# A turned table of weight scales, other transfer costs and a new table of key shifts in a planned attention-plus-FFN kernel

## The chip, the cores and the metric

The kernel runs on one core of a Trainium2 chip. Its metric is the time of one execution in microseconds (us) on that core, as the median of several runs. The engines are TensorE (PE in the profile; PEld is its loading of weights), VectorE (DVE), ScalarE (ACT), GpSimd (POOL) and SyncE (SP, which issues the transfers). Each engine takes its instructions in the order in which they were written into its queue and waits where an operand or a buffer isn't ready.

## The reference

Attention with a threshold (8 batches, 8 heads, 576 positions, head dimension 64), followed by a feed-forward network on 4608 tokens with 512 columns and 2048 hidden units:

```python
scores = scale * np.matmul(q, k.transpose(0, 1, 3, 2))
thresh = np.max(scores, axis=-1, keepdims=True) - tau
scores = np.where(scores >= thresh, scores, -1e9)
attn = np.exp(scores - np.max(scores, axis=-1, keepdims=True))
attn = attn / (np.sum(attn, axis=-1, keepdims=True) + 1e-09)
x = np.matmul(attn, v)              # then (tokens, 512)
h = x @ w_in                        # 512 -> 2048
g = np.where(h >= 1, h, np.where(h <= -1, 0, (h + 1) ** 2 / 4))
out = g @ w_out                     # 2048 -> 512
```

The weights arrive as 8-byte floats; the kernel first turns them into 4-byte floats and then splits them, like every other matmul operand, into a high and a low 2-byte float, so that two or three matmuls stand for one precise one.

## The kernel before

**Attention.** A tile is 128 rows of scores of one head (or 64 rows of each of two heads) against 576 keys; there are 288 tiles, 36 for each batch, and the tiles of a pair of heads form parts. For each tile PE computes the scores `s` (L836; two PSUM buffers, s_61 and s_62 in the order), DVE takes the maximum (L847 to L849), ACT the exponential (L852), DVE applies the threshold and sums (L856), DVE forms the factor (L860, L861), POOL multiplies by it (L864), ACT rounds to the high half (L869), POOL subtracts for the low half (L872), and a transposing transfer issued by SP (L875) writes `eT`. When all tiles of a part are there, PE multiplies by v (L942), and ACT and DVE write the result into the token buffer `x` (L950, L954).

**FFN.** It runs in steps. A step is one block of up to 256 tokens and some hidden units: PE's first matmuls (L1020), on ACT a relu and a square (L1026, L1029), on DVE the gate (L1033), ACT and DVE the halves of g (L1038, L1043), and PE's second matmuls (L1069), which add up in the one PSUM buffer `acc`. The first blocks hold 128 tokens, and a step of theirs has 48 first matmuls of 128 columns.

**Weights.** Each of the 32 blocks of weights (16 of w_in, in tile WI, and 16 of w_out, in WO) is loaded (L630), put together from two words on ACT (L642, L651) and DVE (L656, L660), measured by a small matmul (L667), scaled and split (POOL L721 or L713, PE L733 and L734, ACT L740 or DVE L738).

**Scales.** For w_in a small table `wsc_i` holds, for each of four groups of 512 hidden units, some powers of two; before, it is laid out with the kind of scale outside and the group inside. Once for each batch a block of DVE instructions (`f_scale`, L788 to L796) multiplies four-column rows of that table by the batch's own scale into `fcs`, which the FFN steps of that batch read as scale and bias. The relu of a batch's first step waits for it. Four of the nine instructions have four columns (L791, L793, L794, L795); the others have one. The four read a contiguous row of the table and write every fourth column of `fcs`.

**Order.** The program isn't written in the order in which it runs. Each piece of work becomes an operation with an engine, an estimated cost and a key; `Plan.order()` plays through them with those costs and, whenever an engine is free, takes the ready operation with the smallest key whose buffers are free. `Plan.key()` adds a shift from the table `SHIFT` to the key of single operations (of a kind and a number). Transfers carry a `work` cost in us, with which the planner keeps one clock for all transfers. What comes out is one fixed order for each engine.

Of the kernel before, what the change touches and what calls it, by code (L numbers as in the profile page):

```python
# [27 lines left out]
WL = 3.56  # L28
# [22 lines left out]
SHIFT = {  # L51
    "bits o": {7: -20, 8: -2, 12: -2},
    "den": {73: 5},
    "ffn": {8: 5, 12: -2, 19: 2, 21: -2, 22: -1.71, 23: -5},
    "ffn2": {1: 10, 9: -5, 10: 5, 16: 5, 18: -7.1, 19: -40, 23: -2, 24: 2, 25: -2, 26: -2},
    "load i": {0: -20, 1: -20, 11: -1.07},
    "load o": {8: 2},
    "load q k": {8: 4.48, 10: -4.1},
    "load v": {8: 19.78, 11: 5},
    "low o": {0: -19.88, 1: -18.87, 2: -16.6, 3: -10, 4: -10, 5: -5, 6: -5, 8: -2},  # L60
    "move": {8: -5, 9: -13.89},
    "norm": {39: -2, 58: -2, 69: -2},
    "parts o": {12: -2},
    "q k": {7: 20, 10: -5},
    "q k parts": {1: -8.79, 8: 5, 10: -5},
    "qk": {87: 25.43},
    "scale o": {0: -20},
    "send": {62: -5, 63: -10},
    "tile": {7: -2, 14: -2, 29: 5, 42: -2, 51: -2, 73: -10},
    "v": {1: 5, 2: 5},  # L70
    "v parts": {7: 17.66, 8: 35.35, 9: 33.43, 11: 11.83},
}
# [151 lines left out]
def attn_ffn_kernel(ctx: ExitStack, tc: tile.TileContext, qT, kT, vT, tau, w_in, w_out, out):  # L224
# [9 lines left out]
    NPAIR = H // 2  # L234
# [159 lines left out]
    def add_qk(b, p, need):  # L394
# [90 lines left out]
    def add_v(b, need):  # L485
# [3 lines left out]
        for p in range(NPAIR):  # L489
            rb = plan.buf("raw")  # L490
            bufs.append(rb)

            def load(rb=rb, p=p):
                Y.dma_start(ap(rb, raw), vT[b, 2 * p : 2 * p + 2].rearrange("h d s -> (h d) s"))

            def ssq(rb=rb, p=p):
                A.activation(junk, ap(rb, raw), AF.Square, accum_out=vssq[:, b, p : p + 1])

            l = plan.op("SP", 0.6, plan.key("load v", b * NPAIR + p, need - 8), load, take=[rb], work=1.1, behind=loads[-1] if loads else None)
            loads.append(l)  # L500
            squares.append(plan.op("ACT", 0.67, key - 5, ssq, [l], uses=[rb]))
# [75 lines left out]
    def w_scale(w, n, key, stats, gbuf):  # L577
        sb = plan.buf("ph")
        s = wsc[w][:, :, n]

# [23 lines left out]
    def add_w(w, keys):  # L604
        qn = NU // NQ[w]
        stats = []
        for u in range(NU):
# [82 lines left out]
        for u in range(NU):  # L690
# [5 lines left out]
            src, hi, lo = WT[w][:, u + WOFF, :], WTh[w][:, u, :512], WTh[w][:, u, 512:]  # L696
            s = wsc[w][:, 0, n : n + 1]
            how = CONV[w][u]
# [77 lines left out]
    def ends_():  # L776

        V.tensor_reduce(wsc["i"][:, 8, 0:1], wsc["i"][:, 0], AX.X, ALU.min)
        V.tensor_reduce(wsc["i"][:, 8, 1:2], wsc["i"][:, 1], AX.X, ALU.max)

    wends = plan.op("DVE", 0.13, KI[0] + KI[1] * (NU - 1), ends_, wscale["i"])
    fscale, oscale = {}, {}
    for b in range(B):
        s, f, wi, wo = scs[:, b, :], fcs[:, b], wsc["i"], wsc["o"]

        def f_scale(s=s, f=f, wi=wi):
            u, x, r, rx = (s[:, n : n + 1] for n in (4, 5, 6, 7))
            V.tensor_scalar(r.bitcast(U32), u.bitcast(U32), 1, None, ALU.logical_shift_right)  # L788
            V.tensor_scalar(rx.bitcast(U32), x.bitcast(U32), 1, None, ALU.logical_shift_right)
            V.tensor_scalar(s[:, 0:1], x, 2.0 ** -80, wi[:, 8, 0:1], ALU.mult, ALU.mult)  # L790
            V.tensor_scalar(f[:, :, 0], wi[:, 0], x, 2.0 ** -51, ALU.mult, ALU.mult)  # L791
            V.tensor_scalar(s[:, 0:1], s[:, 0:1], 1.0, 2.0 ** 66, ALU.min, ALU.mult)
            V.tensor_scalar(f[:, :, 1], wi[:, 3], r, 2.0 ** 88, ALU.mult, ALU.mult)  # L793
            V.tensor_scalar(f[:, :, 2], wi[:, 2], rx, 2.0 ** 37, ALU.mult, ALU.mult)  # L794
            V.tensor_scalar(f[:, :, 3], wi[:, 1], u, s[:, 0:1], ALU.mult, ALU.mult)  # L795
            V.tensor_scalar(s[:, 3:4], u, 2.0 ** 65, wi[:, 8, 1:2], ALU.mult, ALU.mult)  # L796

        def o_scale(s=s, wo=wo):
            V.tensor_scalar(s[:, 3:4], s[:, 3:4], 2.0 ** -15, wo[:, 1], ALU.max, ALU.mult)
# [333 lines left out]
```

## Time and profile before

| what | value |
|---|---|
| median of 3 runs | 1152.74 us (1152.41 to 1154.32) |
| the profiled execution | 1154.85 us, its span 1153.0 us |
| PE busy | 1104.0 us of the span (96%) |
| DVE, ACT, POOL busy | 950.2, 898.7, 799.8 us |
| mean granted TensorE clock | 0.986 of full speed |

Busy time of PE is modelled from pipelined matmuls, so it is no measure of how full PE is; the idle time beside it, and the chain of waits, tell where it had nothing to do. A tile's line numbers below are those of the kernel before. The change adds five lines above all the code in question, so that a line of the changed kernel has a number that is five higher (before L791, now L796).

### The profile page before, as it was taken

The numbers are of one execution on the slowest core, as the hardware profiler recorded it, in microseconds if no ns is written. First come the engines' busy times: TensorE is split into PE (matmuls) and PEld (weight loads), VectorE is DVE, ScalarE is ACT, GpSimd is POOL, SyncE is SP. The second block draws the span as 40 slices with busy tenths as digits, with TensorE's granted clock in tenths as the row PEclk, the third lists the DMA queues.
The fourth block names the chain that finished last, engine by engine and source line by source line (L and its number), as shares of the span: only waits on it lengthen the run. The fifth ranks groups of instructions, "written<-read, shape, count | busy, mean of one in ns | idle before, by whom it ended". The sixth has DMA issues, their size and how long they took to land.

```text
span 1153.0 us, 27218 instructions
## 1 busy us (share of the span) xinstructions
PE 1104.0 (96%) x9423; PEld 758.0 (66%) x9423; DVE 950.2 (82%) x2995; ACT 898.7 (78%) x1692; POOL 799.8 (69%) x957
## 2 busy tenths in 40 slices
PE   5789899999999999999999999999999999999998
PEld 3447556767677577676667667676678577676674
DVE  5899988988889989899789888888889889885241
ACT  6989777979788689787888879777888788785362
POOL 3678999588875788668966878758975898654000
PEclk8979999999999999999999999999999999999999
DMA  8798799879895899768995899668996798554000
GB/s 325 275 215 160 125 196 208 162 148 197 155 192 95 177 175 204 146 108 183 187 185 95 161 198 210 121 115 168 201 188 102 150 191 164 108 102 82 19 2 28
DMA packets 435929, 179.40 MB, mean 156 GB/s; under 512 B 400464, under 2 KB 407632, under 8 KB 435792
## 3 DMA queue, kind: packets, MB, share of 16 engines
q1 hardware_dynamic: 435792, 177.67, 76.0%
q8 instruction: 74, 1.21, 0.4%
q14 instruction: 63, 0.52, 0.2%
HBM read 45.09 MB, written 9.44 MB: 47 GB/s over the span
## 4 chain that ended last, share of the span: by engine, by line
PE 54%; DVE 16%; POOL 10%; ACT 8%; issue 6%; DMA 4%; SPq 1%; ACTq 0%; DVEq 0%; POOLq 0%
PE acc L1069 21%; PE ph L1020 20%; PE s L836 7%; PE ph L942 6%; POOL hl L872 3%; DVE e L856 3%; DVE sm L847 3%; POOL e L864 2%; POOL nat L457 2%; ACT e L852 2%; DVE ph L1033 1%; ACT junk L416 1%; DMA eT<-hl 1%; POOL raw L444 1%; DVE ga L1043 1%
## 5 line engine op out<-in xcount | busy, mean ns | idle before, releaser
L872 POOL TENSOR_TENSOR hl<-e,hl 128x576 f16<-128x576 f32 x286 | 366.6, 1286 | 98.7 <-ACT hl L869 95.2
L1020 PE MATMUL ph<-x,WI 128*128 128x256 f16 (+1 forms) x4032 | 401.6, 257 | 1.3 <-DVE gb L1043 0.6
L1020 PEld LDWEIGHTS <-WI 128*128 128x128 f16 x4032 | 346.4, 98 | 53.5 <-issue 5.7
L864 POOL TENSOR_SCALAR e<-e,sm 128x576 f32<-128x576 f32 x286 | 217.5, 765 | 113.0 <-DVE sm L861 76.7
L852 ACT ACTIVATE e<-s,sm,pc 128x576 f32<-128x576 f32 x288 | 237.7, 831 | 55.0 <-DVE sm L848 39.8
L856 DVE SCALAR_TENSOR_TENSOR e<-s,sm,e 128x576 f32<-128x576 f32 x288 | 231.4, 812 | 31.2 <-ACT e L852 24.8
L869 ACT ACTIVATE hl<-e 128x576 f16<-128x576 f32 x286 | 195.0, 684 | 61.0 <-POOL e L864 50.0
L847 DVE TENSOR_REDUCE sm<-s 128x1 f32<-128x576 f32 x288 | 215.6, 749 | 28.1 <-PE s L836 25.9
L836 PE MATMUL s<-kk,qq 128*128 128x288 f16 (+3 forms) x1360 | 193.2, 290 | 18.4 <-DVE e L856 12.5
L1069 PE MATMUL acc<-WO,ga 128*128 128x512 f16 x864 | 207.6, 381 | 0.8 <-ACT ob L1089 0.8
L836 PEld LDWEIGHTS <-qq 128*128 128x128 f16 (+3 forms) x1360 | 113.3, 100 | 94.1 <-issue 47.6
L1033 DVE SCALAR_TENSOR_TENSOR ph<-ph,fcs,asq 128x512 f32<-128x512 f32 (+1 forms) x160 | 112.0, 700 | 53.0 <-ACT asq L1029 52.1
L1026 ACT ACTIVATE asq<-ph,fcs 128x512 f32<-128x512 f32 (+1 forms) x160 | 116.2, 738 | 48.1 <-PE ph L1020 47.5
L1069 PEld LDWEIGHTS <-ga 128*128 128x128 f16 x864 | 81.7, 98 | 83.2 <-issue 4.8
L942 PE MATMUL ph<-eT,vst 128*64 128x320 f16 (+2 forms) x1928 | 124.6, 281 | 3.6 <-DVE WI L656 2.3
L942 PEld LDWEIGHTS <-vst 128*64 128x64 f16 x1928 | 99.3, 111 | 26.9 <-issue 17.4
L1029 ACT ACTIVATE asq<-asq 128x512 f32<-128x512 f32 x144 | 91.0, 632 | 2.1
L1038 ACT ACTIVATE ga<-ph,fcs 128x256 f16<-128x256 f32 (+1 forms) x160 | 70.3, 450 | 25.4 <-DVE ph L1033 23.2
L1043 DVE SCALAR_TENSOR_TENSOR ga<-ph,fcs,ga 128x256 f16<-128x256 f32 (+1 forms) x160 | 70.7, 450 | 21.0 <-ACT WO L1038 7.2
L1069 PE MATMUL acc<-WO,gb 128*128 128x512 f16 x300 | 73.3, 381 | 0.0
L457 POOL TENSOR_TENSOR nat<-raw,nat 128x576 f16<-128x576 f32 x56 | 71.6, 1289 | 1.8 <-ACT nat L450 1.7
L848 DVE TENSOR_SCALAR sm<-sm,pc 128x1 f32<-128x1 f32 x288 | 61.7, 214 | 10.4
(163 smaller groups left out, 1218.5 us busy)
## 6 DMA issues: line engine op xcount, KB each, us to landing
kk<-nat SPq DMA_DIRECT2D x112, 144.0 KB, 2.9
raw<-in_v_dram SPq DMA_DIRECT2D x32, 288.0 KB, 3.5
raw<-in_q_dram SPq DMA_DIRECT2D x32, 288.0 KB, 3.6
raw<-in_k_dram SPq DMA_DIRECT2D x32, 288.0 KB, 3.7
WO<-in_moe_w_in_dram SPq DMA_DIRECT2D x16, 512.0 KB, 8.2
out_dram<-ob SPq DMA_DIRECT2D x32, 256.0 KB, 2.6
qq<-nat SPq DMA_DIRECT2D x112, 72.0 KB, 2.3
x<-in_moe_w_out_dram SPq DMA_DIRECT2D x10, 512.0 KB, 6.0
```

What stands on the lines that cost most here:

```text
L836: T.matmul(ap(s, s_ps)[r, f, :SH], q, k, start=ql == kl == 0, stop=kl == 1)
L847: V.tensor_reduce(t[:, 0:1], sv(), AX.XY, ALU.max, negate=True)
L852: A.activation(halves(ap(e, es)[:, :S]), sv(), AF.Exp, bias=ap(m, sm)[:, 1:2], scale=ap(cb, pc)[:, 24 + v : 25 + v])
L856: V.scalar_tensor_tensor(halves(ap(e, es)[:, :S]), sv(), t[:, 2:3], halves(ap(e, es)[:, :S]), ALU.is_ge, ALU.mult, accum_out=t[:, 3:4])
L864: G.tensor_scalar(ap(e, es)[:, :S], ap(e, es)[:, :S], ap(m, sm)[:, 5:6], 1.0, ALU.mult, ALU.mult)
L869: A.activation(ap(x, hl)[:, :S], ap(e, es)[:, :S], AF.Copy)
L872: G.tensor_tensor(ap(x, hl)[:, w : w + S], ap(e, es)[:, :S], ap(x, hl)[:, :S], ALU.subtract)
L942: T.matmul(o[hd * D : (hd + 1) * D, :n], vt[:, k, hd * D : (hd + 1) * D], t[:, kb, hd * n : (hd + 1) * n], start=m == 0, stop=m == len(blo ...
L1020: T.matmul(h[:, i], WTh["i"][:, u, wl * 512 + c * P : wl * 512 + (c + 1) * P], x[:, cc, xl, c0 : c0 + n].rearrange("p (t n) -> p t n", n=P ...
L1026: A.activation(tv()[:, :, c], hv()[:, :, c], AF.Relu, bias=fcs[:, b, q, 2 : 3], scale=fcs[:, b, q, 1 : 2])
L1033: V.scalar_tensor_tensor(hv()[:, :, c], hv()[:, :, c], fcs[:, b, q, 0 : 1], tv()[:, :, c], ALU.max, ALU.min)
L1069: T.matmul(ap(ab, accs), gv(h, gl)[:, x], WTh["o"][:, fc + i, wl * 512 : (wl + 1) * 512], start=fc + i == 0 and m == 0, stop=fc + i == NFC ...
```

## The change

Three things change; the set of instructions on each engine stays the same in number and kind.

1. The table `wsc` has its two inner dimensions exchanged: the group is outside and the kind of scale inside. The four wide products of `f_scale` now read every ninth column of the table, where before they read four neighbours; they write every fourth column of `fcs`, as before. The two reductions over the groups read with a stride as well. The columns in which two extreme values are kept move along.
2. Costs that only the planner reads: the transfers of k and v 0.88 in place of 1.1, of a block of weights 1.55 in place of 1.75, and `f_scale` 1.2 in place of 1.4.
3. The table `SHIFT` is another one, with 111 entries for 24 kinds of work in place of 63 for 20.

```diff
 SHIFT = {
-    "load i": {0: -20, 1: -20, 11: -1.07},
...
+    "ffn": {3: -40, 4: -40, 5: -2, 7: 10, 11: 40, 17: 20, 19: -20, 20: -19.02},
...
-    wsc = {w: cp.tile([P, 9, NQ[w]], F32, name=f"wsc_{w}") for w in WT}
+    wsc = {w: cp.tile([P, NQ[w], 9], F32, name=f"wsc_{w}") for w in WT}
...
-        lk = plan.op("SP", 0.6, kl, load(kT, rk), take=[rk], work=1.1, behind=lq)
+        lk = plan.op("SP", 0.6, kl, load(kT, rk), take=[rk], work=0.88, behind=lq)
...
-            l = plan.op("SP", 0.6, plan.key("load " + w, u, key - WL), load, before, work=1.75)
+            l = plan.op("SP", 0.6, plan.key("load " + w, u, key - WL), load, before, work=1.55)
...
-        s = wsc[w][:, :, n]
+        s = wsc[w][:, n, :]
...
-        V.tensor_reduce(wsc["i"][:, 8, 0:1], wsc["i"][:, 0], AX.X, ALU.min)
-        V.tensor_reduce(wsc["i"][:, 8, 1:2], wsc["i"][:, 1], AX.X, ALU.max)
+        V.tensor_reduce(wsc["i"][:, 0, 8:9], wsc["i"][:, :, 0], AX.X, ALU.min)
+        V.tensor_reduce(wsc["i"][:, 1, 8:9], wsc["i"][:, :, 1], AX.X, ALU.max)
...
-            V.tensor_scalar(f[:, :, 0], wi[:, 0], x, 2.0 ** -51, ALU.mult, ALU.mult)
+            V.tensor_scalar(f[:, :, 0], wi[:, :, 0], x, 2.0 ** -51, ALU.mult, ALU.mult)
...
-            V.tensor_scalar(f[:, :, 1], wi[:, 3], r, 2.0 ** 88, ALU.mult, ALU.mult)
-            V.tensor_scalar(f[:, :, 2], wi[:, 2], rx, 2.0 ** 37, ALU.mult, ALU.mult)
-            V.tensor_scalar(f[:, :, 3], wi[:, 1], u, s[:, 0:1], ALU.mult, ALU.mult)
+            V.tensor_scalar(f[:, :, 1], wi[:, :, 3], r, 2.0 ** 88, ALU.mult, ALU.mult)
+            V.tensor_scalar(f[:, :, 2], wi[:, :, 2], rx, 2.0 ** 37, ALU.mult, ALU.mult)
+            V.tensor_scalar(f[:, :, 3], wi[:, :, 1], u, s[:, 0:1], ALU.mult, ALU.mult)
...
-        fscale[b] = plan.op("DVE", 1.4, k, f_scale, [VS[b], wends])
+        fscale[b] = plan.op("DVE", 1.2, k, f_scale, [VS[b], wends])
```

Three places of the orders follow; a line of three dots stands for rows left out.

First, DVE at the `f_scale` of the first batch. sm_124 and its like are the small results of one tile, e_94 its exponentials; WO<-x_105 joins two words of a weight. Before:

```order
L656 SCALAR_TENSOR_TENSOR WO<-x_106,ph_65 128x512
...
L856 SCALAR_TENSOR_TENSOR e_94,sm_125<-s_62,sm_125,e_94 128x576
...
L791 TENSOR_SCALAR fcs<-wsc_i,scs 128x4
L792 TENSOR_SCALAR scs<-scs 128x1
L793 TENSOR_SCALAR fcs<-wsc_i,scs 128x4
L794 TENSOR_SCALAR fcs<-wsc_i,scs 128x4
L795 TENSOR_SCALAR fcs<-wsc_i,scs 128x4
...
L847 TENSOR_REDUCE sm_126<-s_61 128x1
```

Now:

```order
L784 TENSOR_REDUCE wsc_i<-wsc_i 128x1
L661 SCALAR_TENSOR_TENSOR WO<-x_105,ph_63 128x512
...
L796 TENSOR_SCALAR fcs<-wsc_i,scs 128x4
L797 TENSOR_SCALAR scs<-scs 128x1
L798 TENSOR_SCALAR fcs<-wsc_i,scs 128x4
L799 TENSOR_SCALAR fcs<-wsc_i,scs 128x4
L800 TENSOR_SCALAR fcs<-wsc_i,scs 128x4
...
L852 TENSOR_REDUCE sm_124<-s_61 128x1
```

The block stood between the fourth tile's threshold and the fifth tile's maximum; it stands ahead of the third tile's maximum now.

Second, PE at the ninth and tenth tile (tile 8 in s_61, tile 9 in s_62; both from kk_78 and qq_82). Before:

```order
L836 MATMUL s_61<-kk_78,qq_82 128x288
...
L667 MATMUL acc<-WO 128x128
L733 MATMUL ph_65<-WI,dgw_132 128x512
L734 LDWEIGHTS minus
L734 MATMUL ph_65<-WI,minus 128x512
...
L836 MATMUL s_62<-kk_78,qq_82 128x288
...
L942 MATMUL ph_63<-eT_99,vst_88 64x128
```

Now:

```order
L672 MATMUL acc<-WO 128x128
L738 MATMUL ph_64<-WI,dgw_132 128x512
L739 LDWEIGHTS minus
L739 MATMUL ph_64<-WI,minus 128x512
...
L841 MATMUL s_61<-kk_78,qq_82 128x288
...
L841 MATMUL s_62<-kk_78,qq_82 128x288
...
L947 MATMUL ph_64<-eT_99,vst_88 64x128
```

The weights' matmuls stood between the scores of the two tiles; they stand ahead of both now.

Third, PE from the third FFN step on (L1020, now L1025; 48 matmuls each). Before:

```order
L1020 MATMUL ph_65<-x_103,WI 128x128
...
L836 MATMUL s_61<-kk_78,qq_82 64x288
...
L1020 MATMUL ph_63<-x_103,WI 128x128
L733 MATMUL ph_64<-WO,dgw_134 128x512
...
L836 MATMUL s_62<-kk_80,qq_84 128x288
```

Now:

```order
L1025 MATMUL ph_63<-x_103,WI 128x128
...
L841 MATMUL s_62<-kk_80,qq_84 128x288
...
L738 MATMUL ph_65<-WI,dgw_133 128x512
...
L1074 MATMUL acc<-WO,ga_110 128x512
...
L841 MATMUL s_61<-kk_79,qq_83 128x288
...
L947 MATMUL ph_63<-eT_99,vst_88 64x320
...
L1025 MATMUL ph_65<-x_103,WI 128x128
```

The fourth step followed the third after the scores of two tiles; now the scores of twelve tiles, the matmuls of the weights and the second matmuls of the first three steps lie between them.

More of the change, by code (lines that the diff above doesn't have):

```diff
@@ L51 @@
 SHIFT = {
[L52 to L55, printed above, removed]
-    "load i": {0: -20, 1: -20, 11: -1.07},
[L57 to L71, printed above, removed]
+    "av": {3: -80, 6: -20, 9: -67.64, 14: 20, 18: 40},
+    "bits o": {15: -20},
+    "den": {33: -80, 35: -40, 38: -10, 41: -2},
+    "ffn": {3: -40, 4: -40, 5: -2, 7: 10, 11: 40, 17: 20, 19: -20, 20: -19.02},
[9 rows of a table added]
+    "move": {5: 17.57, 6: 20},
+    "norm": {7: -2, 12: -10, 13: -20, 14: -20, 16: -40, 20: -20, 31: -80, 38: -2, 43: 5, 59: 5},
[6 rows of a table added]
+    "tile": {13: -2, 14: -5, 36: 10, 42: -2},
+    "v": {1: -1.03, 2: 20},
+    "v parts": {4: -2, 9: 16.66},
+    "x": {10: -5},
 }
@@ L497, in ssq @@
                 A.activation(junk, ap(rb, raw), AF.Square, accum_out=vssq[:, b, p : p + 1])
-            l = plan.op("SP", 0.6, plan.key("load v", b * NPAIR + p, need - 8), load, take=[rb], work=1.1, behind=loads[-1] if loads else None)
+            l = plan.op("SP", 0.6, plan.key("load v", b * NPAIR + p, need - 8), load, take=[rb], work=0.88, behind=loads[-1] if loads else None)
             loads.append(l)
@@ L696, in add_w @@
             src, hi, lo = WT[w][:, u + WOFF, :], WTh[w][:, u, :512], WTh[w][:, u, 512:]
-            s = wsc[w][:, 0, n : n + 1]
+            s = wsc[w][:, n, 0:1]
             how = CONV[w][u]
@@ L789, in f_scale @@
             V.tensor_scalar(rx.bitcast(U32), x.bitcast(U32), 1, None, ALU.logical_shift_right)
-            V.tensor_scalar(s[:, 0:1], x, 2.0 ** -80, wi[:, 8, 0:1], ALU.mult, ALU.mult)
-            V.tensor_scalar(f[:, :, 0], wi[:, 0], x, 2.0 ** -51, ALU.mult, ALU.mult)
+            V.tensor_scalar(s[:, 0:1], x, 2.0 ** -80, wi[:, 0, 8:9], ALU.mult, ALU.mult)
+            V.tensor_scalar(f[:, :, 0], wi[:, :, 0], x, 2.0 ** -51, ALU.mult, ALU.mult)
             V.tensor_scalar(s[:, 0:1], s[:, 0:1], 1.0, 2.0 ** 66, ALU.min, ALU.mult)
[L793 to L796, printed above, removed]
+            V.tensor_scalar(f[:, :, 1], wi[:, :, 3], r, 2.0 ** 88, ALU.mult, ALU.mult)
+            V.tensor_scalar(f[:, :, 2], wi[:, :, 2], rx, 2.0 ** 37, ALU.mult, ALU.mult)
+            V.tensor_scalar(f[:, :, 3], wi[:, :, 1], u, s[:, 0:1], ALU.mult, ALU.mult)
+            V.tensor_scalar(s[:, 3:4], u, 2.0 ** 65, wi[:, 1, 8:9], ALU.mult, ALU.mult)
         def o_scale(s=s, wo=wo):
-            V.tensor_scalar(s[:, 3:4], s[:, 3:4], 2.0 ** -15, wo[:, 1], ALU.max, ALU.mult)
+            V.tensor_scalar(s[:, 3:4], s[:, 3:4], 2.0 ** -15, wo[:, 0, 1:2], ALU.max, ALU.mult)
         k = start[b, 0] + 6
-        fscale[b] = plan.op("DVE", 1.4, k, f_scale, [VS[b], wends])
+        fscale[b] = plan.op("DVE", 1.2, k, f_scale, [VS[b], wends])
         oscale[b] = plan.op("DVE", 0.13, k, o_scale, [fscale[b]] + wscale["o"])
```

15 rows, old and new, of the table SHIFT are left out of this document.

## The prediction

> **What bounds the kernel now.** I read the page first, then busy times by stage, then the chain of waits, then single engines at the places where the chain leaves PE.
>
> The page's row for the engines, and a table of stages (start and end, length, then busy us and instructions of PE, PEld, DVE, ACT and POOL, the granted clock, the transfers' share and GB/s):
>
> ```profile
> PE 1104.0 (96%) x9423; PEld 758.0 (66%) x9423; DVE 950.2 (82%) x2995; ACT 898.7 (78%) x1692; POOL 799.8 (69%) x957
> ```
>
> ```profile
> 0.00:24.00 24.00, 10.43 (x65) 7.91 (x66) 11.68 (x39) 16.91 (x36) 9.11 (x43) 0.96 0.91 339
> 24.00:92.00 68.00, 53.51 (x390) 29.62 (x389) 60.81 (x190) 61.01 (x118) 44.20 (x64) 0.81 0.86 250
> 92.00:216.00 124.00, 115.88 (x1182) 79.87 (x1182) 111.48 (x360) 100.74 (x190) 113.33 (x134) 1.00 0.93 172
> 216.00:384.00 168.00, 167.88 (x1485) 118.27 (x1483) 151.32 (x490) 142.19 (x271) 128.12 (x148) 1.00 0.81 152
> 384.00:408.00 24.00, 21.80 (x150) 12.90 (x149) 20.02 (x62) 14.37 (x27) 14.73 (x14) 0.93 0.89 197
> 408.00:600.00 192.00, 187.85 (x1529) 129.52 (x1527) 167.88 (x528) 157.45 (x294) 151.74 (x178) 1.00 0.87 170
> 600.00:1130.00 530.00, 529.21 (x4553) 372.26 (x4552) 425.93 (x1327) 404.09 (x760) 338.56 (x381) 1.00 0.68 131
> 1130.00:1153.00 23.00, 17.48 (x81) 7.63 (x78) 1.13 (x4) 1.92 (x5) 0.00 (x0) 0.97 0.08 24
> ```
>
> PE is idle for 1153.0 - 1104.0 = 49.0 us. The change moves no work on or off PE, so the time changes by what this idle time changes. It lies in 0 to 24 (13.6 us), 24 to 92 (14.5), 92 to 216 (8.1), 384 to 408 (2.2), 408 to 600 (4.2) and at the very end (5.5, the last eviction and store, which no order helps). From 216 to 384 and from 600 to 1130 PE misses 0.9 us in all: what an order does there is worth nothing.
>
> Up to 24 us everything waits for v and the first weights, and both orders begin alike. From 24 to 92 us DVE (60.8 of 68) and ACT (61.0) set the pace, since PE has no FFN work before the weights are ready. From 92 to 216 us POOL does (113.3 of 124).
>
> The chain of waits (start, length, what), at the pieces that the change touches:
>
> ```profile
> 58.75 0.57 DVE fcs L791
> 59.36 0.62 DVE fcs L793
> 59.98 1.24 DVE fcs L794
> 61.22 0.19 DVE fcs L795
> ...
> 73.33 0.97 PE acc L667 x8
> 74.30 1.81 PE ph L733 x2
> 76.12 0.43 PE ph L734
> 76.54 0.92 PE s L836 x6
> ...
> 124.02 1.21 DVE fcs L794
> 125.23 1.11 DVE fcs L795
> ```
>
> ```profile
> 385.84 1.75 DVE fcs L791
> ...
> 390.04 0.65 PE s L836 x4
> ```
>
> The four-column products of `f_scale` are on the chain three times. They shouldn't be: they handle four numbers for each partition. The instructions in order of time show why they are long:
>
> ```profile
> 58.60 1.36 POOL L721 TENSOR_SCALAR WI<-WI,wsc_i 128x512 f16<-128x512 f32 x2
> 58.66 0.65 DVE L791 TENSOR_SCALAR fcs<-wsc_i,scs 128x4 f32<-128x4 f32 x1
> 59.22 0.14 DVE L792 TENSOR_SCALAR scs<-scs 128x1 f32<-128x1 f32 x1
> ...
> 59.88 1.34 DVE L794 TENSOR_SCALAR fcs<-wsc_i,scs 128x4 f32<-128x4 f32 x1
> 59.92 1.27 POOL L872 TENSOR_TENSOR hl<-e,hl 128x576 f16<-128x576 f32 x1
> ```
>
> L794 ends at 61.22, POOL's L872 at 61.19; L791 ends at 59.31, and POOL's two L721 together at 59.96, so the first of them at about 59.3. A four-column product lasts until POOL's instruction of that moment is over; the one-column L792 between them is not held (0.14). Where POOL doesn't interfere, the same products take this:
>
> ```profile
> 894.34 0.21 DVE L793 TENSOR_SCALAR fcs<-wsc_i,scs 128x4 f32<-128x4 f32 x1
> 894.47 0.22 DVE L794 TENSOR_SCALAR fcs<-wsc_i,scs 128x4 f32<-128x4 f32 x1
> 894.60 0.28 DVE L795 TENSOR_SCALAR fcs<-wsc_i,scs 128x4 f32<-128x4 f32 x1
> ```
>
> One starts 0.13 us after the other.
>
> **The change part by part.** The turned table. It takes away nothing by itself; what it can do is end the holding. Its two ends: if a product with a stride on both sides isn't held, it costs its 0.13 us (L795 0.19, as on the chain at 61.22). First batch: 0.57 + 0.62 + 1.24 - 3 x 0.13 = 2.0 us. Second batch: 1.21 + 1.11 - 0.13 - 0.19 = 2.0 us. Batch at 385.84: 1.75 - 0.13 = 1.6 us, and there PE itself stood still behind it:
>
> ```profile
> 390.04 0.65 PE L836 MATMUL s<-kk,qq 128*128 128x288 f16 x4 [2.20 <-DVE e L856]
> ```
>
> Together 5.6 us; the five other batches' blocks lie in stretches in which PE doesn't wait. The other end is 0: the products are held as before. For the upper end speaks that a one-column product beside them is free, so that holding hangs on the shape of the operands, and the operand that was contiguous is the one that changes; against it, that the output had a stride already. No row shows a product with two strides. I take the 5.6, as only slightly likelier than 0, since it decides more of the result than any other term.
>
> Planner's costs and keys. They do nothing on the chip but set the order. I counted, for fixed points of the program, the instructions ahead of them on an engine in both orders. Four things follow.
>
> (a) Two waits of DVE between 24 and 92 us:
>
> ```profile
> 44.55 0.69 DVE L656 SCALAR_TENSOR_TENSOR WI<-WO,ph 128x512 uint32<-128x512 uint32 x1 [1.79 <-ACT ph L651]
> ...
> 77.49 0.76 DVE L847 TENSOR_REDUCE sm<-s 128x1 f32<-128x576 f32 x1 [1.13 <-PE s L836]
> ```
>
> The second is the second place of the order: between the scores of tiles 8 and 9 PE did 0.97 + 1.81 + 0.43 = 3.2 us of weights' matmuls, and DVE waited for tile 9. With both tiles' scores side by side that work is behind DVE's work on tile 8, so 1.13 us go. The first: ACT came late with a word of one of the last blocks of w_in. In the new order ACT's L651 of these blocks stand further ahead (the fifteenth is ACT's instruction 50, before 59), so I take its 1.79 us as gone too. Together 2.9 us, between 0 and 2.9 us if something else is late there.
>
> (b) What DVE has to do before the first FFN step. It can begin when `x` has been written by the fourth L954. Ahead of that now stand one L528 (the low half of a later batch's v), one L656, one L660 and five operations of one column more, and the maximum, mask and four small operations of one tile less; the small ones cancel to within 0.1 us:
>
> ```profile
> L528 DVE SCALAR_TENSOR_TENSOR vb<-raw,scs,vb 128x576 f16<-128x576 f32 x28 | 35.6, 1272 | 0.3 <-POOL vb L523 0.2
> L656 DVE SCALAR_TENSOR_TENSOR WI<-WO,ph 128x512 uint32<-128x512 uint32 x11 | 7.4, 681 | 3.3 <-ACT ph L651 3.3
> L847 DVE TENSOR_REDUCE sm<-s 128x1 f32<-128x576 f32 x288 | 215.6, 749 | 28.1 <-PE s L836 25.9
> L856 DVE SCALAR_TENSOR_TENSOR e<-s,sm,e 128x576 f32<-128x576 f32 x288 | 231.4, 812 | 31.2 <-ACT e L852 24.8
> ```
>
> 1.27 + 2 x 0.68 - 0.75 - 0.81 = 1.1 us later (L660 does the same columns as L656 and is taken as equal). Behind L954 PE waits with the first L1020.
>
> (c) The first `f_scale` moves ahead of the third tile. All of its nine instructions come before tiles 2 and 3 and not after; DVE does the same sum, and the first relu that needs it is far behind in both orders. Its cover is that DVE never idles there, so I count 0.
>
> (d) The FFN steps behind the third. This is the third place of the order. Ahead of the first scores of the second batch (tile 36) stood seven steps' first matmuls (336), and now stand five (240), with as many second matmuls (36); one pair of L733 and L734 less as well. What moves behind, by the same work where it stood before:
>
> ```profile
> 104.43 2.84 PE L1020 MATMUL ph<-x,WI 128*128 128x128 f16 x48
> ...
> 110.04 2.85 PE L1020 MATMUL ph<-x,WI 128*128 128x128 f16 x48
> 112.73 1.08 PE L733 MATMUL ph<-WO,dgw 128*128 128x512 f32 x2
> ...
> 118.87 1.12 PE L733 MATMUL ph<-WO,dgw 128*128 128x512 f32 x2 [1.82 <-DVE x L954]
> ```
>
> 2.84 + 2.85 + 1.1 = 6.8 us of PE's work. If tile 36 comes when it came before, PE has idled that much longer, and from 216 us on it has no slack to make it good: 6.8 us is the upper end. The lower end is 0, if the attention comes that much sooner. For POOL, which paces 92 to 216, exactly the same instructions stand ahead of the low half of tile 36 in both orders, and POOL idles only 124.0 - 113.3 = 10.7 us there. But what stands ahead of the earlier tiles on POOL is more now (at the seventeenth low half one L457, one L523 and two L864), so that some of POOL's later work is done in its idle time before 92 us (24.0 - 9.1 and 68.0 - 44.2, together 38.7 us). That leaves room to come sooner by most of 6.8 us. I take 1.8 us, a wait as the longest of PE's in that stretch.
>
> Sum: -5.6 - 2.9 + 1.1 + 1.8 = -5.6 us. The profiled execution, 1154.85 us (its span and 1.85 us around it), would become 1149.2; it was 2.1 us above the median of the runs, so for the median 1152.74 - 5.6 = 1147.1 us.
>
> [...]
>
> **The rivals.** The products are held as before. Mechanism: a stride on one operand didn't free them, so neither does a stride on the other, and each of the four still lasts until POOL's current instruction ends. For it speaks L794's 1.34 us with its strided output; against it only that a second stride is new. Time: -2.9 + 1.1 + 1.8 = 0.0, so 1152.7 us, no change; it can go either way by a us or two, since the blocks meet POOL at other moments.
>
> PE runs short between 92 and 216 us (slower). Place: behind the third FFN step. The price is the full 6.8 us in place of 1.8. It decides from the point at which tile 36 comes no sooner than before. For it speaks that POOL has the same work ahead of that tile, and that DVE and ACT have little slack before 92 us (7.2 and 7.0 of 68 us); against it POOL's idle 38.7 us. With the products held: -2.9 + 1.1 + 6.8 = +5.0, 1157.7 us. With the products free it would be -0.6, no change.
>
> The order's gain isn't there. The waits of (a) go but others come, and the products are free: -5.6 + 1.1 + 1.8 = -2.7, 1150.0 us. It is the upper part of the forecast's own range.
>
> **How the numbers follow.** Of a single measurement, 0.2% (2.3 us) is about what can be told from no change. Forecast (products free, a modest price in (d)): 0.44, nearly all of it faster by more than 2.3 us (0.41), the rest within; its own range is 1143 to 1151. Products held: 0.28, within 2.3 us mostly (0.15), faster 0.07, slower 0.06. PE short: 0.28, slower 0.25, within 0.03. Sums: faster 0.48, same 0.21, slower 0.31. The range must reach to the last case: 1142 to 1158 us; about 0.1 is left out on either side.
>
> **What would show it.** The products: their groups' means near 0.2 us and none of them on the chain, or means of 0.4 to 0.7 as now. (a): no wait of DVE for L651's or PE's scores above 1 us between 24 and 92 us. (d): PE's busy time from 92 to 216 us, 115.9 now; below 112 would show the second rival, and 216 to 384 us would again have no idle time. PE's idle time over the span, 49.0 us now, must fall to about 43. The forecast is wrong if this idle time grows, or if it falls while the groups' means of the products stay.

## The result and the profile after

The change makes the kernel slower. Beside each other on the chip the changed kernel took 1159.9 us (median of 4 runs, 1155.65 to 1161.56) and the kernel before 1152.6 us (4 runs, 1151.54 to 1154.32); the ratio is 1.0053, with a 95% interval of 1.0032 to 1.0074. The prediction had said 1147.1 us, and 1159.9 lies above its whole range.

The profiled execution of the changed kernel is the shortest of its four (1155.65 us, span 1153.9 us). It is used for where waits lie and how long they are; times are compared by the ratios. The page's row of engines, after:

```profile
PE 1098.7 (95%) x9423; PEld 758.2 (66%) x9423; DVE 957.1 (83%) x2995; ACT 901.5 (78%) x1692; POOL 797.7 (69%) x957
```

PE's idle time, which the prediction wanted to see fall from 49.0 to about 43 us, has grown to 1153.9 - 1098.7 = 55.2 us. The span of these two profiles grew by 0.9 us only, since PE's busy time, which is modelled, is 5.3 us less here for the same 9423 matmuls. So the idle time shows where PE waits, and isn't by itself the size of the loss. Where PE is idle, the table of stages after says (the columns as in the prediction's table):

```profile
24.00:92.00 68.00, 47.26 (x384) 26.36 (x385) 63.19 (x195) 61.23 (x119) 45.61 (x65) 0.77 0.85 253
92.00:216.00 124.00, 113.37 (x1138) 77.08 (x1137) 113.19 (x354) 99.59 (x184) 115.06 (x145) 0.97 0.86 170
384.00:408.00 24.00, 22.58 (x159) 14.16 (x158) 22.92 (x76) 16.90 (x33) 17.84 (x23) 1.00 0.85 164
408.00:600.00 192.00, 190.31 (x1562) 132.93 (x1560) 165.54 (x522) 159.15 (x297) 150.38 (x177) 1.00 0.86 176
600.00:1130.00 530.00, 527.88 (x4549) 371.80 (x4548) 428.08 (x1334) 405.11 (x758) 338.89 (x382) 1.00 0.67 131
```

From 24 to 92 us PE idles 20.7 us where it idled 14.5, although DVE does more there (63.19 us for 60.81). From 92 to 216 us it idles 10.6 for 8.1 us, and from 600 to 1130 us 2.1 for 0.8. It is better from 384 to 408 us, 1.4 for 2.2 us, and from 408 to 600 us, 1.7 for 4.2 us.

Of the long waits of PE from 24 us on that the kernel before hasn't got, these four are followed below, in order of time; two more (2.30 us at 30.31 us and 2.42 us at 171.67 us) are not. A second profile of the same program, taken later, has neither the wait at 171.67 us nor the one at 151.26 us:

```profile
58.12 0.61 PE L672 MATMUL acc<-WO 128*128 128x128 bf16 x4 [6.05 <-DVE WO L661]
99.34 1.81 PE L947 MATMUL ph<-eT,vst 128*64 128x128 f16 x30 [2.58 <-DVE wsc_o L327]
151.26 1.63 PE L841 MATMUL s<-kk,qq 64*128 64x288 f16 x12 [2.84 <-DVE e L861]
915.24 0.65 PE L841 MATMUL s<-kk,qq 128*128 128x288 f16 x4 [1.84 <-DVE e L861]
```

All four end with DVE. What DVE does ahead of the first of them, with POOL's instructions of the same moment between (instructions of both engines in order of time, changed kernel):

```profile
52.77 1.22 DVE L799 TENSOR_SCALAR fcs<-wsc_i,scs 128x4 f32<-128x4 f32 x1
52.80 1.16 POOL L718 TENSOR_TENSOR WI<-WI 128x512 f16<-128x512 f32 x1
53.90 1.32 DVE L800 TENSOR_SCALAR fcs<-wsc_i,scs 128x4 f32<-128x4 f32 x1
53.91 1.28 POOL L462 TENSOR_TENSOR qq<-raw,qq 128x576 f16<-128x576 f32 x1
...
55.25 0.74 DVE L852 TENSOR_REDUCE sm<-s 128x1 f32<-128x576 f32 x1
...
56.35 0.75 DVE L852 TENSOR_REDUCE sm<-s 128x1 f32<-128x576 f32 x1
...
57.39 0.68 DVE L661 SCALAR_TENSOR_TENSOR WO<-x,ph 128x512 uint32<-128x512 uint32 x1
```

Two things are to be seen. The products are held as before: L799 ends 0.03 us after POOL's L718, L800 0.03 us after L462, with a stride on both operands. And the first `f_scale`, which now stands ahead of the third tile's maximum, takes from 51.33 to 55.33 us, 4.0 us; the word of w_out (L661) that PE's small matmul L672 wants comes behind it and two tiles' maxima, and PE, which takes its instructions in order, stands for 6.05 us.

### The profile page after: what moved, and what is told of

Same layout as the page of the kernel before. It is cut to its first block, busy times and chain, and to the rows that moved or that the text cites. A ratio compares the mean times of both kernels' runs of the same rounds, so it can differ in the third digit from the quotient of the medians.

```text
span 1153.9 us, 27249 instructions
## 1 busy us (share of the span) xinstructions
PE 1098.7 (95%) x9423; PEld 758.2 (66%) x9423; DVE 957.1 (83%) x2995; ACT 901.5 (78%) x1692; POOL 797.7 (69%) x957
## 4 chain that ended last, share of the span: by engine, by line
PE 62%; DVE 14%; POOL 6%; issue 4%; ACT 4%; DMA 2%; SPq 1%; ACTq 0%; POOLq 0%; DVEq 0%
PE acc L1074 24%; PE ph L1025 22%; PE s L841 8%; PE ph L947 7%; DVE e L861 3%; DVE sm L852 3%; POOL hl L877 2%; POOL e L869 2%; DVE ph L1038 1%; POOL nat L462 1%; DVE ga L1048 1%; ACT e L857 1%; DVE sm L853 1%; ACT hl L874 1%; DMA eT<-hl 1%
## 5 line engine op out<-in xcount | busy, mean ns | idle before, releaser
L877 POOL TENSOR_TENSOR hl<-e,hl 128x576 f16<-128x576 f32 x286 | 367.1, 1290 | 107.8 <-ACT hl L874 105.6
L1025 PE MATMUL ph<-x,WI 128*128 128x256 f16 (+1 forms) x4032 | 402.7, 258 | 0.7 <-DVE x L959 0.7
L1025 PEld LDWEIGHTS <-WI 128*128 128x128 f16 x4032 | 348.1, 98 | 52.9 <-issue 5.2
L869 POOL TENSOR_SCALAR e<-e,sm 128x576 f32<-128x576 f32 x286 | 216.5, 762 | 109.0 <-DVE sm L866 81.9
L861 DVE SCALAR_TENSOR_TENSOR e<-s,sm,e 128x576 f32<-128x576 f32 x288 | 230.7, 812 | 24.7 <-ACT e L857 17.9
L841 PE MATMUL s<-kk,qq 128*128 128x288 f16 (+3 forms) x1360 | 188.1, 291 | 11.1 <-DVE e L861 8.5
L462 POOL TENSOR_TENSOR nat<-raw,nat 128x576 f16<-128x576 f32 x56 | 71.1, 1282 | 2.4 <-ACT nat L455 2.3
```

Source lines behind the costliest of these rows:

```text
L841: T.matmul(ap(s, s_ps)[r, f, :SH], q, k, start=ql == kl == 0, stop=kl == 1)
L861: V.scalar_tensor_tensor(halves(ap(e, es)[:, :S]), sv(), t[:, 2:3], halves(ap(e, es)[:, :S]), ALU.is_ge, ALU.mult, accum_out=t[:, 3:4])
L869: G.tensor_scalar(ap(e, es)[:, :S], ap(e, es)[:, :S], ap(m, sm)[:, 5:6], 1.0, ALU.mult, ALU.mult)
L877: G.tensor_tensor(ap(x, hl)[:, w : w + S], ap(e, es)[:, :S], ap(x, hl)[:, :S], ALU.subtract)
L1025: T.matmul(h[:, i], WTh["i"][:, u, wl * 512 + c * P : wl * 512 + (c + 1) * P], x[:, cc, xl, c0 : c0 + n].rearrange("p (t n) -> p t n", n=P ...
```

## The experiments

The first theory, formed from these rows: the turned table does nothing, and the order loses, because the `f_scale` blocks now stand ahead of work for which PE waits and are lengthened by POOL. The rival: the table itself costs. In all the runs below a kernel is timed in five rounds beside the kernel before.

### The two halves of the change

Table alone: the kernel before with the new layout of `wsc`, the old keys and costs. Order alone: the new keys and costs with the old layout.

```diff
-    wsc = {w: cp.tile([P, 9, NQ[w]], F32, name=f"wsc_{w}") for w in WT}
+    wsc = {w: cp.tile([P, NQ[w], 9], F32, name=f"wsc_{w}") for w in WT}
```

> The kernel before with the turned table alone; order and costs are the old ones. Theory (the loss lies in the order): no change, 1152.6 us within 2 us, and the four-column products still last until POOL's instruction ends, with group means of 0.4 to 0.7 us as before. Rival (the table itself costs, because a strided source makes the held products longer): the whole loss is here, about 1158 to 1160 us, with longer means of the products.

> The changed kernel with the table as it was, so that only the order (keys and planner's costs) is new. Theory (the loss lies in the order): as the changed kernel, 1158 to 1160 us, ratio about 1.005, with the long wait of PE for DVE's word of the output weights (6.05 us at 58 us) again. Rival (the table costs): 1152.6 us, no change.

> The changed kernel once more, for a second profile and for how far its runs lie apart. Theory: ratio 1.003 to 1.007 again; the profile shows the same waits of PE as the first one (6.05 us at 58 us for DVE's word of the output weights). If the first profile was a lucky one, as its time of 1155.7 against a median of 1159.9 suggests, this one has PE idle for more than 55 us, and the place where it is longer shows what differs from run to run.

Table alone: ratio 0.9991 (0.9974 to 1.0008). Order alone: 1.0056 (1.0037 to 1.0075). The changed kernel again: 1.0052 (1.0036 to 1.0068), median 1157.2 us, profile 1151.5 us long. The second row of products, in the kernel with the turned table alone and in the changed kernel (least, median and greatest duration in ns, first and last start; the kernel before has 215/222/1259):

```profile
L793 DVE TENSOR_SCALAR fcs<-wsc_i,scs x8: 216/222/1257, 58.8 to 889.0; 128x4 f32<-128x4 f32 x8
```

```profile
L798 DVE TENSOR_SCALAR fcs<-wsc_i,scs x8: 216/724/1274, 52.2 to 909.1; 128x4 f32<-128x4 f32 x8
```

The loss is the order's alone, and the table does nothing, neither good nor harm. The order alone had the 6 us wait again (6.25 us, at 58.06 us).

### Products that are not held

Each product is read as three rows of two overlapping columns (0 1, 1 2, 2 3) and written as six columns, so that the outermost counts are 3 and 6; the readers take columns 0, 1, 3 and 5. Six elements in place of four, the same number of instructions; `fcs` has six columns for each batch now, and room for five batches in turn in place of eight, in this and in the other forms below. That counts of 3 and 6 free a product no row had shown before this run. Of this form, in the old order, I expected means of 0.2 to 0.3 us, none over 0.4, and 3 to 5.6 us less, 1147 to 1149.5 us; of five columns read and five written, that they are held and the time stays.

```diff
+        return bass.AP(t.tensor, t.offset, [[p, P], [d, 3], [d, 2]])
...
-            V.tensor_scalar(f[:, :, 0], wi[:, 0], x, 2.0 ** -51, ALU.mult, ALU.mult)
+            V.tensor_scalar(f[:, :, 0], three(wi[:, 0]), x, 2.0 ** -51, ALU.mult, ALU.mult)
```

> The kernel before, with each four-column product written as three rows of two overlapping columns into six columns (six elements, of which two are repeats), so that the outermost counts of source and output are 3 and 6. [...] Rival 1 (every product of more than one column is held): means of 0.4 to 0.7 us as before, 1152.6 us. Rival 2 (free, but the time that is won goes to the next wait): means of 0.2 to 0.3 us and 1151.5 to 1152.6 us.

> The kernel before with six-element products as in the run that freed them, but read as two rows of three overlapping columns in place of three rows of two; the output's six columns, the number of instructions and of elements are the same. Theory (a product is held when the outermost counts of source and output are both even or equal): 2 and 6 are even, so the products are held as in the kernel before, medians of 0.3 to 0.7 us with some above 1.2 us, and the time is that of the kernel before, within 0.2%. Rival (what freed them was the second dimension, the overlap or the six elements): all near 0.22 us, and ratio about 0.9955.

> The kernel before with products of five columns (the fifth is the next row's first, and isn't used), five in the source and five in the output. [...] Rival (any odd count is free): all near 0.22 us, ratio about 0.9955.

The same product with three rows of two, with two rows of three (0 1 2, 1 2 3, outermost counts 2 and 6), and with five columns read and five written, each in the old order:

```profile
L800 DVE TENSOR_SCALAR fcs<-wsc_i,scs x8: 211/214/216, 58.3 to 887.7; 128x6 f32<-128x6 f32 x8
```

```profile
L800 DVE TENSOR_SCALAR fcs<-wsc_i,scs x8: 218/222/1260, 59.2 to 891.9; 128x6 f32<-128x6 f32 x8
```

```profile
L800 DVE TENSOR_SCALAR fcs<-wsc_i,scs x8: 214/220/1255, 59.1 to 891.8; 128x5 f32<-128x5 f32 x8
```

The greatest of eight is what to look at: 216 ns with three rows, 1260 and 1255 ns with the other two forms. The times go with it: 0.9955 (0.9937 to 0.9973), 0.9987 (0.9969 to 1.0006), 0.9992 (0.9976 to 1.0009). So it is neither the number of elements nor the second dimension nor the overlap that frees a product, since two rows of three have all of these and are held, but how the columns are split: with outermost counts (source and output) of 4 and 4 (1259 ns), 2 and 6, and 5 and 5 it is held here, with 3 and 6 it isn't. No run has other counts.

In the old order all eight blocks of `f_scale`, from the first of their nine instructions to the end of the last, take 3.1, 3.1, 1.1, 3.7, 3.0, 1.1, 2.3 and 1.4 us, 18.8 together; with free products each takes 1.1. PE's wait of 2.20 us at 390.04 us, a term of the prediction, is gone, and PE's scores at that place follow the work before them with no wait (kernel with free products, PE in order of time):

```profile
387.55 2.78 PE L1027 MATMUL ph<-x,WI 128*128 128x256 f16 x24
390.17 0.65 PE L843 MATMUL s<-kk,qq 128*128 128x288 f16 x4
```

The run was repeated twice beside other kernels, with 0.9957 (0.9941 to 0.9974) and 0.9933 (0.9912 to 0.9954):

> The kernel before with free products once more, beside the changed order with free products on the same chip. Theory: ratio 0.994 to 0.997 again.

> The old order with free products beside them on the same chip: ratio 0.994 to 0.997, as twice before.

The mean of the three, 0.9948, is 6 us less than the kernel before. This version beats both kernels.

### Free products and the place of f_scale in the new order

Four kernels in the new order: with free products; with the first `f_scale` moved on DVE to where it stood before, products held; with the second one moved as well, behind the scale factors of w_out; and with both moved and the products free.

```diff
+        todo = plan.order()
+        for moved, ahead in [(1141, 1190), (1143, 1308)]:
+            o = next(x for x in todo if x.n == moved)
+            todo.remove(o)
+            todo.insert(next(i for i, x in enumerate(todo) if x.n == ahead) + 1, o)
```

> The changed kernel with the products in six elements, three rows of two, as in the run of the kernel before that freed them. Theory (the new order's PE waits of 6.05 us at 58 us and 2.58 us at 99 us are DVE's f_scale blocks, 3.9 and 2.35 us long because POOL holds their products): the blocks take about 1.1 us, the waits become about 3.2 and 1.3 us, and the time falls by 4 to 6 us, to about 1152 us, ratio to the kernel before 0.999 to 1.002. With products free in both, the new order would still be about 6 us behind the old one (1146 us). Rival (the order's loss lies elsewhere and the products are hidden in this order): about 1157 us, ratio 1.004 to 1.006.

> The changed kernel with one operation moved on DVE: the first f_scale stands again where it stood before, behind the threshold and exponent sum of the fourth tile (the products are held as in the changed kernel). Theory (the step that the prediction counted 0, f_scale ahead of the third tile, makes PE's 6.05 us wait): DVE's word of w_out comes 3.9 us sooner, the wait at 58 us becomes about 2.2 us, and the time falls by 2 to 4 us, to 1153.5 to 1155.5 us. Rival (the wait is the early matmuls on w_out, and PE would have nothing to do there anyway): PE's wait is shorter, but another of the same length comes right behind it, 1157 to 1159 us.

> The same, and the second f_scale moved behind the scale factors of w_out (L595 to L600 on DVE), which PE's second-longest new wait, 2.58 us at 99 us, is for. Theory: this wait falls to about 0.2 us and the clock, 0.50 for 4 us behind it, stays at 1.00, so 3 to 5 us less than with the first one alone: 1149 to 1152 us. Rival: only the wait itself goes, or not even that, because POOL paces 92 to 216 us: within 2 us of the run with the first one alone.

> Both: products free and both f_scale blocks moved back, in the changed kernel's order. Theory (held products and the place of f_scale are the whole of the order's loss): as the kernel before with free products, 1146 us, ratio 0.994 to 0.997. Rival (the early matmuls on w_out and the later FFN steps cost by themselves): 1149 to 1153 us, ratio 0.998 to 1.001, and PE's busy time from 92 to 216 us below 116 us.

PE's first two new waits with free products, and with the first block moved back:

```profile
54.63 0.61 PE L672 MATMUL acc<-WO 128*128 128x128 bf16 x4 [3.33 <-DVE WO L661]
...
94.44 1.03 PE L954 MATMUL ph<-eT,vst 128*64 128x128 f16 x30 [1.30 <-DVE wsc_o L327]
```

```profile
54.18 0.60 PE L672 MATMUL acc<-WO 128*128 128x128 bf16 x4 [2.33 <-DVE WO L661]
...
97.42 1.81 PE L947 MATMUL ph<-eT,vst 128*64 128x128 f16 x30 [2.94 <-DVE wsc_o L327]
```

The waits came out as expected to 0.2 us or less: 6.05 becomes 3.33 and 2.33 (expected 3.2 and 2.2), 2.58 becomes 1.30 (expected 1.3). The times: free products 0.9963 (0.9943 to 0.9983), first block back 1.0026 (1.0010 to 1.0041), both back 1.0026 (1.0007 to 1.0045), both back and free 0.9949 (0.9930 to 0.9969). So moving the first block back takes away half of the order's loss, 0.27% or 3.1 us, and freeing the products more than all of it. Each ratio is known to about 0.2% only, and the two cures overlap: at its old place the first block is also held less, 2.9 us long in place of 4.0. Moving the second one gave nothing, though its wait fell to 0.98 us: a miss. Both cures together came to the old order with free products (0.9948), as the theory of that run had it.

Why free products bring more in the new order shows far behind the places that the prediction looked at. The blocks take 4.0, 2.4, 2.5, 3.8, 1.6, 1.4, 1.1 and 4.4 us there, 21.2 together for 18.8 in the old order. The second half of the last, in the changed kernel, with POOL beside it:

```profile
909.73 1.34 DVE L799 TENSOR_SCALAR fcs<-wsc_i,scs 128x4 f32<-128x4 f32 x1
909.76 1.28 POOL L462 TENSOR_TENSOR nat<-raw,nat 128x576 f16<-128x576 f32 x1
...
910.98 1.32 DVE L800 TENSOR_SCALAR fcs<-wsc_i,scs 128x4 f32<-128x4 f32 x1
911.00 1.28 POOL L877 TENSOR_TENSOR hl<-e,hl 128x576 f16<-128x576 f32 x1
```

The block met four POOL instructions in a row, and PE's wait of 1.84 us at 915.24 us is behind it. The last block of the old order took 1.4 us and nobody waited. With free products the new order has no wait there either.

### What is left with free products

The new order with free products again, first beside the old one and then beside the last kernel of this section:

> The changed kernel with free products once more, on the same chip as the old order with free products. Theory (with free products the two orders are worth the same, the order's loss being the held products at their new places): ratio 0.994 to 0.998, within 0.2% of the old order. Rival (the new order costs 0.1 to 0.3% by itself): ratio 0.997 to 0.999, 2 to 3 us above the old order.

> The changed order with free products beside it on the same chip: ratio 0.996 to 0.999, as twice before.

0.9987 (0.9966 to 1.0009) and 0.9972 (0.9949 to 0.9994). With 0.9963 the mean is 0.9974, against 0.9948 for the old order: 0.26%, 3 us, is what the new order still loses; by the intervals of the six runs this difference lies between 0.1 and 0.4%. Part of it may again be the place of `f_scale`, since the kernel with free products and both blocks moved back had 0.9949; but a second run of it, with one more move (below), had 0.9966, so that isn't shown. One candidate was the third new wait. DVE's L533, the low half of a pair of the second batch's v, and POOL beside it, changed kernel:

```profile
143.68 6.79 DVE L533 SCALAR_TENSOR_TENSOR vb<-raw,scs,vb 128x576 f16<-128x576 f32 x1
150.39 0.81 DVE L861 SCALAR_TENSOR_TENSOR e<-s,sm,e 128x576 f32<-128x576 f32 x1
```

```profile
143.31 1.49 POOL L869 TENSOR_SCALAR e<-e,sm 128x576 f32<-128x576 f32 x2
144.74 1.30 POOL L877 TENSOR_TENSOR hl<-e,hl 128x576 f16<-128x576 f32 x1
145.99 0.72 POOL L726 TENSOR_SCALAR WO<-WO,wsc_o 128x512 f16<-128x512 f32 x1
146.65 2.54 POOL L877 TENSOR_TENSOR hl<-e,hl 128x576 f16<-128x576 f32 x2
149.14 0.72 POOL L726 TENSOR_SCALAR WO<-WO,wsc_o 128x512 f16<-128x512 f32 x1
```

An instruction whose median is 0.97 us (28 of them) lasted until POOL's run of instructions was over, and the masks L861 behind it came some 5 us late. The second profile of the same program had it at 3.11 us. To test it, L533 was put behind the masks and sums of the two tiles it stood ahead of:

```diff
+        for moved, ahead in [(187, 1461)]:
```

> The changed order with free products, and one operation moved on DVE: the low half of one pair of the second batch's v (L533 of the changed kernel, 6.8 us long at 144 us in its profile, since six of POOL's instructions in a row go ahead of it) is put behind the masks and sums of the two tiles it stood ahead of. Theory (this is the part of the new order's loss that free products leave): PE's 2.8 us wait for DVE's masks at 145 to 151 us goes, and the kernel comes to the old order with free products, ratio 0.994 to 0.997, within 0.1% of that run. Rival (the rest lies in the two FFN steps that come later or in the early words of w_out): within 1 us of the changed order with free products, ratio 0.997 to 0.999, and PE waits as long elsewhere before 216 us.

> The changed kernel with the low half of v moved alone; the products are held. Theory: PE's 2.84 us wait at 151 us goes, 2 to 3 us less than the changed kernel, ratio 1.002 to 1.0035. Rival: 1.0045 to 1.006, as the changed kernel.

> The changed order with free products, both f_scale blocks moved back, and the low half of v moved. Theory: nothing more than the low half of v gives, since the blocks are 1.1 us long now: ratio 0.993 to 0.996. If the early place of the f_scale blocks costs by itself, this is 1 to 2 us below the run without that move.

Measured: 0.9979 (0.9965 to 0.9993) with free products, 1.0041 (1.0022 to 1.0061) with held ones, 0.9966 (0.9950 to 0.9982) with free products and the blocks moved. None of them can be told from the same kernel without the move (0.9974, 1.0053 and 0.9949), so the move wins nothing, and the theory as it stood falls. Where the wait went, the kernel with free products shows (DVE and then PE):

```profile
148.00 2.58 DVE L533 SCALAR_TENSOR_TENSOR vb<-raw,scs,vb 128x576 f16<-128x576 f32 x1 [2.50 <-DMA raw<-in_q_dram]
```

```profile
154.04 0.89 PE L848 MATMUL s<-kk,qq 64*128 64x288 f16 x6 [2.34 <-DVE e L868]
```

L533 takes 2.58 us there and not 6.79, but DVE is idle for 2.5 us before it and for 2.44 us before the second tile's mask, and PE waits 2.34 us for the next tile's masks. The long instruction had mostly filled a gap. That doesn't clear it: in two profiles of the order without the move it lasted 3.1 us, and each is the shortest of its kernel (span 1151.5 us against 1153.9 with held products, 1141.2 against 1146.3 and 1148.1 with free ones). Whether that is its doing isn't shown.

The second candidate was w_out. With free products PE is busy 49.29 us from 24 to 92 us in the new order and 56.92 in the old one, and its longer waits there in the new one are mostly for the words of w_out, of which one to three more stand ahead of the fifth to the thirteenth tile's maxima on DVE. The rows of the key table for w_out alone were set back:

```diff
-    "low o": {0: -59.43, 1: -40, 2: -39.08, 3: -35.66, 4: -40, 5: -10, 6: -10, 7: -5, 8: -5, 11: -2},
+    "low o": {0: -19.88, 1: -18.87, 2: -16.6, 3: -10, 4: -10, 5: -5, 6: -5, 8: -2},
...
```

> The changed order with free products, and in the table of keys the rows for w_out alone (bits, fix, load, low, parts and scale of o) as they were before; DVE's words of w_out then stand later: 7 of the 16 ahead of the tenth tile's maximum, where the changed order has 13 and the old one 10. Theory (what free products leave of the new order's loss is w_out's words and their Gram matmuls ahead of the first tiles, for which PE waits 8.9 us in all between 54 and 81 us): these waits shrink by half and the ratio comes to 0.993 to 0.996. Rival (the two FFN steps that come later, or the whole of the keys together): ratio 0.997 to 1.000, PE's waits between 50 and 90 us shorter all the same.

1.0107 (1.0074 to 1.0140): 15 us worse than the new order with free products, and not better. PE's waits above 0.8 us for w_out from 58 to 92 us are gone, but two for DVE's masks, of 2.92 and 2.31 us, stand in their place; the table of stages of that kernel:

```profile
24.00:92.00 68.00, 49.62 (x379) 30.86 (x380) 59.67 (x197) 60.04 (x114) 46.56 (x65) 0.73 0.78 241
92.00:216.00 124.00, 110.12 (x1064) 72.71 (x1062) 103.17 (x333) 97.33 (x178) 109.02 (x134) 0.93 0.86 170
```

From 92 to 216 us PE now is busy for 110.12 us only, and its second matmuls, which need w_out, begin at 134.9 us, where they began at 115.4. The whole order changes with these keys, so this run doesn't isolate the early words; it suggests that the rest of the new table relies on them. What makes the last 0.26% stays open.

## Why the prediction was wrong, step by step

**Products freed, -5.6 us.** This step failed: the change doesn't free them (0.9991 with the table alone), and the first rival's condition was the true one (its time, no change, came out for the table alone and not for the whole change). No row before the change showed a product with two strides, and the one stride that a row did show, that of L794's output, hadn't kept it from lasting 1.34 us; that two strides free a product was my estimate, and I still set the two at nearly even odds. The price was right as a sum: in the old order products that really are free gave 0.45, 0.43 and 0.67%, 5.2, 5.0 and 7.7 us.

**(c) The first f_scale moved, counted 0.** This is the second step that failed, and the one that turned the sign: 0.27% or 3.1 us, half of the loss. The cover that the prediction named, that DVE never idles there, is no cover. DVE, busy for 63.19 of the 68 us there, sets the pace, so what stands ahead of a word on its queue delays whoever waits for that word (PE, for 6.05 us); the sum of DVE's work was right and its sequence was what mattered. A further part of the loss is the same mechanism at other places: the held blocks meet longer runs of POOL in the new order, one of them at 908 us, where the prediction had said that an order is worth nothing. Freeing the products gives 0.9948 in the old order and takes the new one from 1.0053 to 0.9974, 0.79 for 0.52%. The difference of 0.27% is what holding costs the new order beyond the old one, half of its loss too; since the first block's long stay at its early place is part of both halves, they can't simply be added.

**(a) Two waits of DVE gone, -2.9 us.** The waits did go: DVE has none above 0.9 us from 24 to 92 us, and is busy 2.4 us longer. On DVE this even came out: its fourth write into `x` (L954, now L959), which (a) and (b) together put 1.8 us sooner, begins at 90.82 us for 92.34, 1.5 us sooner. But PE didn't win it, and its idle time there grew by 6.2 us. The prediction counted idle time of DVE as time of the path without asking for whom PE waits on the way; in the new order that is mostly the words of w_out.

**(b) DVE's work ahead of the first FFN step, +1.1 us.** The first FFN matmul begins at 91.75 us after and at 92.68 before, 0.9 us sooner and not 1.1 later:

```profile
91.75 0.44 PE L1025 MATMUL ph<-x,WI 128*128 128x128 f16 x5
```

```profile
92.68 0.49 PE L1020 MATMUL ph<-x,WI 128*128 128x128 f16 x6 [0.28 <-DVE x L954]
```

By itself (b) can't be told from (a), whose gain lies ahead of the same matmul. That the changed kernel is slower although its FFN begins sooner shows that this start was no measure of PE's time.

**(d) Two FFN steps put off, +1.8 us of 0 to 6.8.** Tile 36's maximum begins at 172.3 us in the changed kernel's first profile and 166.1 in its second, against 164.7 before, though two steps fewer stand ahead of it. By the prediction's own rule (the full price, if that tile comes no sooner) this is the upper end, which was the second rival. That rival with held products gave 1157.7 us, the nearest of all to what was measured. Its sign, PE busy below 112 us from 92 to 216, didn't show (113.4, and 116.1 in the second profile), and no run isolates the steps. They may be the open 0.26%; that isn't shown.

So the measured +0.53%, some 6 us, is about 3 us that go when the products are freed, beyond what freeing wins in the old order, and about 3 us that stay, where the prediction's terms for the order gave 0.0. The first block's early place, counted 0, is the one single move whose cost the runs show.

## What to carry to other kernels

A small instruction that another engine can hold (here 0.22 us by itself, up to 1.34 us beside POOL) is priced by what runs beside it and by what is queued behind it, not by its size: look where an order puts it, and at every place where it occurs. Before counting on a layout to free it, have a run that shows such a layout free; here three rows of two into six columns were (216 ns at most in the second row of products, where the three other forms had 1255 to 1260), at no cost in instructions. On an engine that never idles, ask who waits for what a move puts back before counting it as free.

## What the runs showed of the hardware

**Passed over.** DVE's L533 reads two tiles, raw and vb. It began at 143.68 us in the changed kernel, and six POOL instructions that began after it (the second L869 up to the L726 at 149.14) were done before it, each in its usual time (0.75, 1.30, 0.72, 1.27, 1.27 and 0.72 us, where the means of their groups are 0.76, 1.29 and 0.71); it ended at 150.47, 0.6 us after the last. In the second profile of the same program two were (the second L869 and L877), and it ended 0.8 us after them:

```profile
142.23 3.11 DVE L533 SCALAR_TENSOR_TENSOR vb<-raw,scs,vb 128x576 f16<-128x576 f32 x1
```

```profile
144.51 1.30 POOL L726 TENSOR_SCALAR WO<-WO,wsc_o 128x512 f16<-128x512 f32 x1
```

There POOL's L726 took 1.30 us in place of 0.72: this time POOL's instruction was the longer one. The four-column products that are held end with POOL's current instruction (L799 and L800 0.03 us after it); L533 didn't, it lasted through six more. What decides which of two instructions is done first isn't shown.

**A pause can be paid twice.** Behind several of PE's long waits the granted clock is at 0.50 for some us. So it is around the wait of 6.25 us that ends at 58.06 us in the run of the order alone, and around the wait of 2.58 us that ends at 99.34 us in the changed kernel (four-us slices):

```profile
48.00:52.00 4.00, 2.32 (x20) 1.16 (x18) 3.86 (x19) 4.00 (x9) 3.82 (x9) 1.00 0.80 297
52.00:56.00 4.00, 0.00 (x0) 0.00 (x0) 3.94 (x7) 1.19 (x3) 4.00 (x5) 0.50 0.84 313
56.00:60.00 4.00, 1.94 (x6) 1.00 (x7) 3.89 (x12) 3.65 (x6) 1.27 (x3) 0.50 0.17 49
```

```profile
96.00:100.00 4.00, 1.42 (x39) 1.35 (x35) 3.83 (x17) 3.06 (x7) 4.00 (x5) 0.87 0.19 41
100.00:104.00 4.00, 4.00 (x42) 3.00 (x39) 3.90 (x16) 4.00 (x9) 2.43 (x5) 0.50 0.70 132
```

(In the changed kernel the clock is at 0.50 from 48 us on already, ahead of its wait of 6.05 us.) The length of a wait alone doesn't decide. With free products the wait at the second place is 1.30 us. In the first profile of that kernel the clock's mean from 96 to 104 us is 1.00, in the second 0.57. In the run with L533 moved as well, whose order is the same up to there, it is 0.58 behind the same 1.30 us, and the 48 first matmuls of the next FFN step take nearly twice as long (that first profile, then this run):

```profile
97.00 2.85 PE L1032 MATMUL ph<-x,WI 128*128 128x128 f16 x48
```

```profile
98.92 5.28 PE L1032 MATMUL ph<-x,WI 128*128 128x128 f16 x48
```

The same wait of 2.8 us near 150 us, too, left the clock at 1.00 in the changed kernel and at 0.50 in the run of its order alone. What decides isn't shown. The prediction had priced waits at their own length.
